# A gated-recurrence and expert-routing kernel: the path for very full experts as one loop, column numbers made a step before their conversion, and a fourth buffer of rows

## The chip, the cores and the metric

The kernel runs on one NeuronCore of a Trainium2 chip. The metric is device time in microseconds (us) of one execution, the median of three runs. The engines of the core are named as in the profile: PE is TensorE (PEld its weight loads), DVE VectorE, ACT ScalarE, POOL GpSimd, SP SyncE, which here issues most transfers. [...] records of a sequencer carry a q (PEq, ACTq).

## What is computed

Two stages follow each other. The first is a gated linear recurrence over 768 steps for 4 x 8 heads of 48 channels; the second routes each of the 3072 resulting rows of 384 values to one of 8 experts by cosine similarity, and applies that expert's two-layer network. The reference, cut to what matters:

```python
for t in range(S):                                   # B, H, S, D = 4, 8, 768, 48
    state = alpha[:, :, t, :, None] * state + einsum('bhd,bhe->bhde', k[:, :, t], v[:, :, t])
    y[:, :, t] = einsum('bhd,bhde->bhe', q[:, :, t], state)

x = y.transpose(0, 2, 1, 3).reshape(B * S, H * D)    # 3072 x 384
xn = x / (norm(x) + 1e-6);  en = expert_emb / (norm(expert_emb) + 1e-6)
logits = xn @ en.T / tau
expert_idx = argmax(logits, axis=1)                  # 8 experts
gate_w = softmax(logits)[arange(N), expert_idx]
for e in range(E):
    mask = expert_idx == e
    h = maximum(x[mask] @ w1[e], 0.0)                # 384 -> 1024
    out[mask] = gate_w[mask, None] * (h @ w2[e])     # 1024 -> 384
```

How many rows an expert gets depends on the data. With the reference's inputs the eight experts get 418, 365, 379, 426, 395, 371, 351 and 367 rows.

## The kernel before

The recurrence is done in 24 steps of 128 rows (`NS = 24`), software-pipelined over a loop `s`. Rows come out of step `s` two iterations later, are collected in tiles `x` for groups of one to three steps, get their expert (`choose`), their place in a list sorted by expert (`place`), and are sent to that list in DRAM by an indirect transfer from GpSimd (`to_rows`).

```python
    S0, EARLY = 16, 2
    # the groups of steps:
    # (0,3) (3,6) (6,9) (9,12) (12,14) (14,16) (16,19) (19,21) (21,23) (23,24)

    def routing_constants():
        nc.gpsimd.memset(ones, 1.0)
        make_upper_triangular(nc, earlier, val=1.0, diag=False)
        nc.gpsimd.iota(cols_i, pattern=[[1, E]], base=0, channel_multiplier=0)
        # ... three more iotas: toks_i, part_i, starts_i
        for f, i in ((cols, cols_i), (toks, toks_i), (part, part_i), (starts, starts_i)):
            nc.vector.tensor_copy(f, i)
        nc.vector.tensor_scalar(first, cols, -1.0, float(E), ALU.mult, ALU.add)
        nc.vector.tensor_scalar(ebase, cols, float(N), None, ALU.mult)
        nc.vector.tensor_scalar(before[:, 0], ebase, 1.0 / P, None, ALU.mult)
```

`before[:, s]` holds, per partition, how many rows of earlier steps chose each expert. `choose` ends with these additions; `place` multiplies them on TensorE (`rk`), and for steps 15 and 23 the total too:

```python
        def choose(g):
            # ... top, win, best and chosen, all on VectorE
            for s in range(s0, s1):
                eng = nc.vector if s == NS - 1 else nc.gpsimd
                eng.tensor_tensor(before[:, s + 1], before[:, s], chosen[:, s], ALU.add)

        def place(g, total=False):
            mm(rkf, lhsT=ones, rhs=before[:, s0:s1]..., start=True, stop=False)
            mm(rkf, lhsT=earlier, rhs=ch..., start=False, stop=True)
            if total:
                mm(bank[:, GMAX], lhsT=ones, rhs=before[:, s1], start=True, stop=True)
            # ... at_row, row and dest on VectorE

        def rows(s):
            # ... TensorE writes px, 128 rows of the step, into one of 3 PSUM buffers ("tr"),
            #     which the transposes pa, pk, pq, pkb of later steps use too
            if s == s0:
                x_g[g] = work.tile([P, GMAX, ROW], FP32, name="x", bufs=3)[:, 0 : s1 - s0]
            x = x_g[g][:, s - s0]
            nc.vector.tensor_reduce(x[:, LG : LG + E]..., px[...], axis=AX.XY, op=ALU.add)
            nc.scalar.copy(x[:, 0:DM]..., px[...])

        for s in range(NS + 3):
            # ... the work of the steps s, s - 1 and s - 2
            if s == 3:
                with behind(s):          # behind step s's second scan and its qs on GpSimd
                    routing_constants()
```

The experts then run one after another. Each has three blocks of 128 rows (`run`) and, if it has more than 384, a half block of 64 (`run_extra`, under a `tc.If`). Once, behind the fourth expert, stands a path for experts with more than 448 rows:

```python
        def half_block(w1_t, w2_t, xT, gate, col):
            # ... 48 matmuls ph, 8 matmuls pyo
            nc.scalar.copy(y[0:HALF], py[HALF:])
            nc.vector.tensor_tensor(y[0:HALF], y[0:HALF], py[0:HALF], ALU.add)
            nc.vector.tensor_scalar(y[0:HALF], y[0:HALF], gate, None, ALU.mult)
            scatter(y[0:HALF], col)

        def run_rest(free):
            w1_t, w2_t = w1_s[free], w2_s[free]
            big = nc.values_load(most, ...)          # half blocks over 384 of the fullest expert
            with tc.If(big > 1):
                for i in range(E):                   # eight copies in the program
                    e = nc.values_load(turn_i[0:1, i : i + 1], engines=(SP,), ...)
                    # ... load w1_t and w2_t of expert e
                    n = nc.values_load(extra[0:1, i : i + 1], ...)
                    with tc.For_i(1, n) as u:
                        # ... load 64 rows, transpose, gates
                        half_block(w1_t, w2_t, xT, gate[0:HALF], col[0:HALF])

        for i in range(E):
            # ... weights(i + 2) and fetch(i + 2)
            run(i)
            run_extra(i)
            if i == 3:
                run_rest(i % NW)
```

Of the kernel before, what the change touches and what calls it, by code (L numbers as in the profile page):

```python
# [9 lines left out]
FP32 = mybir.dt.float32  # L10
# [17 lines left out]
def kernel(  # L28
# [40 lines left out]

    xs = nc.dram_tensor("xs", (E * N + NROW, ROW), FP32, kind="Internal").ap()  # L70

    consts = ctx.enter_context(tc.tile_pool(name="consts", bufs=1))


# [36 lines left out]
# [4 lines that stand above are left out]
        nc.gpsimd.iota(toks_i, pattern=[[P, NS]], base=1, channel_multiplier=1)  # L115
        nc.gpsimd.iota(part_i, pattern=[[0, 1]], base=0, channel_multiplier=1)
        nc.gpsimd.iota(starts_i, pattern=[[P, NC + 1]], base=0, channel_multiplier=0)
        for f, i in ((cols, cols_i), (toks, toks_i), (part, part_i), (starts, starts_i)):
            nc.vector.tensor_copy(f, i)
        nc.vector.tensor_scalar(first, cols, -1.0, float(E), ALU.mult, ALU.add)  # L120
        nc.vector.tensor_scalar(ebase, cols, float(N), None, ALU.mult)
        nc.vector.tensor_scalar(before[:, 0], ebase, 1.0 / P, None, ALU.mult)
# [73 lines left out]
    with ExitStack() as c1:  # L196
# [123 lines left out]
        def choose(g):  # L320

            s0, s1 = GROUPS[g]
            n = s1 - s0
            shp = [P, n, E]
            l = x_g[g][:, :, LG : LG + E]
            top = work.tile([P, GMAX], FP32, name="top")[:, 0:n]
            nc.vector.tensor_reduce(top.unsqueeze(2), l, axis=AX.X, op=ALU.max)
            win = work.tile([P, GMAX, E], FP32, name="win")[:, 0:n]
            nc.vector.tensor_tensor(win, l, bc(top, shp, 2), ALU.is_equal)
            nc.vector.tensor_tensor(win, win, bc(first, shp, 1), ALU.mult)  # L330
            best = work.tile([P, GMAX], FP32, name="best")[:, 0:n]
            nc.vector.tensor_reduce(best.unsqueeze(2), win, axis=AX.X, op=ALU.max)  # L332
            ch = chosen[:, s0:s1]
            nc.vector.tensor_tensor(ch, win, bc(best, shp, 2), ALU.is_equal)
            for s in range(s0, s1):
                eng = nc.vector if s == NS - 1 else nc.gpsimd
                eng.tensor_tensor(before[:, s + 1], before[:, s], chosen[:, s], ALU.add)

        def place(g, total=False):
# [114 lines left out]
        def behind(s):  # L454

            queue = ExitStack()
            for call in st[s]["last"]:
                queue.enter_context(tc.issue_after(call.ins))
            return queue
# [149 lines left out]
        def rows(s):  # L609

            yT = st[s]["yT"]
            px = ps_tr.tile([P, 2, NQ, 2 * D + E], FP32, tag="tr", name="px")
            for hh in range(2):
                for q in range(NQ):

                    for i in range(2):
                        sl = slice(i * HALF, (i + 1) * HALF)
                        mm(
                            px[sl, hh, q], lhsT=yT[hh][:, q, sl], rhs=sel[:, hh, q],
                            start=True, stop=True, skip_group_check=True,  # L620
                        )
            g = group_of[s]
            s0, s1 = GROUPS[g]
            if s == s0:
                x_g[g] = work.tile([P, GMAX, ROW], FP32, name="x", bufs=3)[:, 0 : s1 - s0]
            x = x_g[g][:, s - s0]
            nc.vector.tensor_reduce(  # L627
                x[:, LG : LG + E].unsqueeze(2), px[:, :, :, 2 * D :].rearrange("t a q e -> t e a q"),
                axis=AX.XY, op=ALU.add,
            )  # L630
            nc.scalar.copy(  # L631
                x[:, 0:DM].rearrange("t (q j a d) -> t a q j d", q=NQ, j=2, a=2),
                px[:, :, :, 0 : 2 * D].rearrange("t a q (j d) -> t a q j d", j=2),
            )
# [36 lines left out]
        for s in range(NS + 3):  # L671
            if s + 2 <= NS:
                load(s + 2)
            if 0 <= s - 1 < NS:
                with in_turn():
                    keys_back(s - 1)
            if s < NS:
                decays(s)
            if s == NS:
                with in_turn():  # L680
                    turn_early()
            if s < NS:
                decay_queries(s)
            if 0 <= s - 1 < NS:
                decay_state(s - 1)

                with in_turn(), tc.issue_after(st[s]["a_scan"].ins) if s < NS else ExitStack():
                    scores(s - 1)
            if s == 0:
                with behind(s), in_turn():  # L690
                    prepare_first(a0)
                with behind(s):
                    prepare_logits()
            if NS <= s < NS + 2:
                with in_turn():
                    first_layer_early(2 * (s - NS), 2 * (s - NS) + 1)
            if 0 <= s - 2 < NS:
                with in_turn():
                    mix_states(s - 2)
                with in_turn():  # L700
                    mix_chunk(s - 2)
            if 0 <= s - 1 < NS:

                with in_turn(), tc.issue_after(st[s]["a_scan"].ins) if s < NS else ExitStack():
                    update(s - 1)
            if 0 < s < NS and s % NCH == 0:

                with in_turn():
                    keys_back(s, ps_mm, "mm")
            if NS <= s < NS + 2:  # L710
                with in_turn():
                    first_layer_early(2 * (s - NS) + 1, 2 * (s - NS) + 2)
            if 0 <= s - 2 < NS:
                with in_turn():
                    rows(s - 2)
            if s == 1:
                with in_turn():
                    turn_logits()
            if s == 3:
                with behind(s):  # L720
                    routing_constants()
            if 4 <= s < 4 + NXG * (NC + 1):
                i, t = divmod(s - 4, NC + 1)
                with behind(s):
                    nc.gpsimd.memset(xg_s[i][:, t], 0.0)
            if s == 3:
                with behind(s):
                    nc.gpsimd.memset(blank, 0.0)

            r = s - 3  # L730
            if r >= 0:
                g = group_of[r]
                if r == GROUPS[g][1] - 1:
                    with in_turn():
                        n = place(g, r in (S0 - 1, NS - 1))
                    if r == S0 - 1:
                        with behind(s):
                            first_expert(n)
            with behind(s) if s < NS else ExitStack():
                for c in send[:] if s >= NS else send[:1]:  # L740
                    to_rows(dest[:, c : c + 1], x_g[group_of[c]][:, c - GROUPS[group_of[c]][0]])
                    send.remove(c)
                    if c == S0 - 1:
                        fetch_early()
                        weights(0)
            if s == NS - 1:
                weights(1)
            r = s - 2
            if 0 <= r < NS:
                g = group_of[r]  # L750
                if r == GROUPS[g][1] - 1:
                    choose(g)
                    with behind(s) if s < NS else ExitStack():
                        nc.gpsimd.tensor_copy(x_g[g][:, :, TK], toks[:, slice(*GROUPS[g])])
            if s > NS:
                with in_turn():
                    first_layer_early(2 * (s - NS) + 2, 2 * (s - NS) + 4)
# [6 lines left out]
    with ExitStack() as c3:  # L764
# [164 lines left out]
        def run_rest(free):  # L929
# [4 lines left out]
                skip_runtime_bounds_check_because="the half blocks of an expert",  # L934
            )
            with tc.If(big > 1):  # L936
                for i in range(E):
                    e = nc.values_load(
                        turn_i[0:1, i : i + 1], engines=(SP,), min_val=0, max_val=E - 1,
                        skip_runtime_bounds_check_because="a sum of two experts, less E from E on",  # L940
                    )
                    nc.sync.dma_start(
# [3 lines left out]
                        out=w2_t, in_=w2_r[ds(e, 1)].rearrange("e p k d -> (e p) k d")  # L946
                    )
                    n = nc.values_load(
                        extra[0:1, i : i + 1], min_val=0, max_val=N // HALF - 2 * NC,
                        skip_runtime_bounds_check_because="the half blocks of an expert",  # L950
                    )
                    with tc.For_i(1, n) as u:
# [64 lines left out]
```

## Time and profile before

| | |
|---|---|
| time, median of 3 (lowest to highest) | 451.35 us (451.18 to 452.82) |
| span of the profiled execution | 451.3 us, granted TensorE clock 0.987 on average |
| DMA traffic | 60.10 MB, 133 GB/s over the span |
| matmuls of the experts, L843 and L854 | 120.8 + 115.6 us busy |
| VectorE's two scans in a step, L474 and L498 | 24 times 1.22 us each |
| GpSimd's scatter of 128 rows, L309 | 24 times 1.03 us |

The profile is one execution. Its page gives busy times by engine, the span in 40 equal slices (a digit is the busy share in tenths; PEclk is the clock that TensorE was granted, in tenths of full speed), the groups of instructions by source line, and the chain of work that ended last. The trace behind it can be asked who waited for whom, and for single instructions in order of time. A line such as `L936 ACTq COMPARE_BRANCH  x1: 45/45/45, 303.2 to 303.2` is a group of records: line, sequencer, operation, count, shortest/median/longest in ns, first and last start in us.

### The profile page before, as it was taken

What the parts mean: (1) busy time and instruction counts of PE and PEld (TensorE: products, weight loads), DVE (VectorE), ACT (ScalarE), POOL (GpSimd) and SP (SyncE); (2) the same over time, 40 slices, a digit from 0 to 9 for tenths busy, and PEclk for the clock granted to TensorE, in tenths of its full rate; (3) what the DMA queues carried; (4) which work ended last, traced back from release to release, by engine and by line L of the source; (5) the groups of instructions that cost most, each with busy time, mean ns of one, the idle gap of its engine ahead of it and who ended that gap; (6) DMA issues with size and microseconds to landing.
All of it is one profiled execution on the core that took longest, in us unless ns stands there. A gap on an engine that the chain in (4) does not pass through costs nothing.

```text
span 451.3 us, 9164 instructions
## 1 busy us (share of the span) xinstructions
PE 431.3 (96%) x3474; PEld 301.0 (67%) x3474; DVE 172.5 (38%) x464; ACT 154.7 (34%) x330; POOL 138.3 (31%) x230
## 2 busy tenths in 40 slices
PE   7989999999999999999999999988999999999992
PEld 6878888888788876765555555545556655655551
DVE  7878878788788344220211211110111121121010
ACT  4444444544454436622502413311421250250200
POOL 7455667676466445010010110102010001001010
PEclk9999999999999999999999999998999999999997
DMA  9999999999839825863045054008204500000000
GB/s 142 157 162 175 197 192 164 205 189 173 164 104 316 311 75 165 330 231 137 20 169 207 19 197 173 17 21 307 62 35 162 192 17 35 0 19 33 0 20 33
DMA packets 119369, 60.10 MB, mean 133 GB/s; under 512 B 102287, under 2 KB 113816, under 8 KB 119312
## 3 DMA queue, kind: packets, MB, share of 16 engines
q1 hardware_dynamic: 115208, 49.14, 46.9%
q0 software_dynamic: 3728, 10.16, 6.3%
q8 instruction: 34, 0.56, 0.5%
q14 instruction: 23, 0.19, 0.1%
q10 hardware_dynamic: 376, 0.05, 0.1%
HBM read 49.69 MB, written 11.45 MB: 135 GB/s over the span
## 4 chain that ended last, share of the span: by engine, by line
issue 53%; PE 26%; DVE 7%; POOL 5%; DMA 4%; another core or an unknown queue 2%; ACT 1%; POOLq 1%; DVEq 0%; ACTq 0%
PE pyx L187 6%; PE sc L187 4%; POOL out_dram L781 3%; PE px L187 3%; PE pyo L854 2%; PE pa L190 2%; PE pq L190 2%; PE pk L190 2%; PE pkb L190 2%; DVE r L474 2%; PE phe L187 2%; PE pd L187 1%; DMA xs<-x,dest 1%; DMA out_dram<-y,sx 1%
## 5 line engine op out<-in xcount | busy, mean ns | idle before, releaser
L843 PE MATMUL ph<-xT,w 128*128 128x384 f32 (+1 forms) x384 | 120.8, 466 | 3.8 <-ACTq L936 3.2
L854 PE MATMUL pyo<-w,hT 128*128 128x384 f32 x352 | 115.6, 488 | 0.0
L843 PEld LDWEIGHTS ph<-xT,w 128*128 128x128 f32 x384 | 68.4, 192 | 46.9 <-issue 5.7
L854 PEld LDWEIGHTS pyo<-w,hT 128*128 128x128 f32 x352 | 66.3, 190 | 45.3
L781 POOL DMA_INDIRECT out_dram<-y,sx x25 | 24.4, 977 | 229.3 <-DVE gt L824 135.2
L847 ACT ACTIVATE hT<-ph 128x384 f32<-128x384 f32 (+1 forms) x64 | 29.7, 465 | 141.4 <-PE ph L843 141.4
L797 DVE COPY xT<-pxg 128x384 f32<-128x384 f32 (+1 forms) x30 | 15.0, 504 | 95.5 <-PE pxg L796 95.5
L858 DVE TENSOR_SCALAR y<-pyo,gt 128x384 f32<-128x384 f32 (+1 forms) x22 | 13.4, 609 | 85.3 <-PE pyo L854 85.3
L502 POOL TENSOR_TENSOR qs<-qc,a 128x512 f32<-128x512 f32 x24 | 30.6, 1276 | 34.0 <-DVE a L498 24.1
L474 DVE TENSOR_TENSOR_SCAN r<-pa,inr 128x511 f32<-128x511 f32 x24 | 29.2, 1215 | 5.7 <-PE pa L190 5.5
L498 DVE TENSOR_TENSOR_SCAN a<-pa,ini 128x512 f32<-128x512 f32 x24 | 29.3, 1222 | 0.8
L309 POOL DMA_INDIRECT xs<-x,dest x24 | 24.8, 1032 | 11.2 <-DVE best L332 4.0
L187 PE MATMUL sc<-qs,kr 64*128 64x128 f32 x384 | 28.1, 286 | 0.0
L187 PE MATMUL pyx<-sm,vt 128*64 128x128 f32 x384 | 26.5, 279 | 0.2 <-POOL sm L568 0.2
L187 PEld LDWEIGHTS sc<-qs,kr 64*128 64x128 f32 x384 | 23.5, 189 | 4.2 <-issue 3.4
L187 PEld LDWEIGHTS pyx<-sm,vt 128*64 128x64 f32 x384 | 20.4, 136 | 4.4 <-issue 3.3
L607 ACT COPY ycols<-pyx 128x256 f32<-128x256 f32 x48 | 17.8, 374 | 13.9 <-PE pyx L187 12.5
L187 PE MATMUL px<-sel,ycols 128*64 128x104 f32 x384 | 21.5, 254 | 0.0
L484 ACT COPY qc<-pq 128x512 f32<-128x512 f32 x24 | 14.1, 586 | 21.2 <-PE pq L190 21.2
L631 ACT COPY x<-px 128x384 f32<-128x384 f32 x24 | 11.6, 484 | 25.5 <-DVE x L627 25.5
L567 ACT COPY sm<-sc 128x512 f32<-128x512 f32 x24 | 14.1, 587 | 13.5 <-PE sc L187 12.9
L187 PEld LDWEIGHTS px<-sel,ycols 128*64 128x64 f32 x384 | 17.7, 137 | 1.2 <-issue 0.7
(164 smaller groups left out, 504.4 us busy)
## 6 DMA issues: line engine op xcount, KB each, us to landing
w<-in_moe_w_dram SPq DMA_DIRECT2D x16, 1536.0 KB, 6.7
kt<-in_k_dram SPq DMA_DIRECT2D x24, 192.0 KB, 4.3
qt<-in_q_dram SPq DMA_DIRECT2D x24, 192.0 KB, 5.6
vt<-in_v_dram SPq DMA_DIRECT2D x24, 192.0 KB, 5.5
xg<-xs SPq DMA_DIRECT2D x22, 196.5 KB, 7.8
at<-in_alpha_dram SPq DMA_DIRECT2D x24, 168.0 KB, 5.7
xg<-xs SPq DMA_DIRECT2D x8, 98.2 KB
at<-in_alpha_dram SPq DMA_DIRECT2D x24, 22.5 KB, 5.2
```

What stands on the lines that cost most here:

```text
L187: last["pe"] = nc.tensor.matmul(*args, **kwargs)
L190: last["pe"] = nc.tensor.transpose(*args)
L309: ins = nc.gpsimd.indirect_dma_start(out=xs, out_offset=bass.IndirectOffsetOnAxis(ap=rows, axis=0), in_=x, in_offset=None, bounds_check=E ...
L474: nc.vector.tensor_tensor_scan(r[:, L - 2 :: -1], pa[:, L - 1 : 0 : -1], inr[:, L - 2 :: -1], 1.0, ALU.mult, ALU.add,)
L498: d["a_scan"] = by_dve = nc.vector.tensor_tensor_scan(a, pa, ini, 0.0, ALU.mult, ALU.add)
L502: by_pool = nc.gpsimd.tensor_tensor(qs.rearrange("p n t -> p (n t)"), d["qc"], a, ALU.mult)
L607: nc.scalar.copy(yT[hh].rearrange("p q t -> p (q t)"), pyx[hh][:, 0:YX])
L781: ins = nc.gpsimd.indirect_dma_start(out=out, out_offset=bass.IndirectOffsetOnAxis(ap=col, axis=0), in_=y, in_offset=None, bounds_check=N - 1,
L797: return nc.vector.tensor_copy(xT, px[:, :, 0:n])
L843: nc.tensor.matmul(ph, lhsT=w1_t[:, i, f * P : (f + 1) * P], rhs=xT[:, i], start=(i == 0), stop=(i == KT - 1),)
L847: return nc.scalar.activation(hT[:, f], ph, AF.Relu)
L854: nc.tensor.matmul(py, lhsT=hT[:, f], rhs=w2_t[:, f], start=(f == 0), stop=(f == FT - 1),)
```

## The change

There are four parts. The path for experts with very many rows becomes one run-time loop over the experts (`tc.For_i`) in place of eight copies in the program; [...] `extra` and `turn_i` are first written to DRAM, and each pass loads its two numbers from there. GpSimd's numbering of the columns (`iota`) is issued one step ahead of VectorE's conversion to float, so that VectorE need not wait for it. The addition that feeds the total after step 15 goes to VectorE. And the tile of rows `x` has four buffers in place of three, so that a group need not wait for the scatter of the group three before it.

```diff
+    turns = nc.dram_tensor("turns", (2, E), I32, kind="Internal").ap()
...
         nc.gpsimd.iota(starts_i, pattern=[[P, NC + 1]], base=0, channel_multiplier=0)
+
+    def convert_constants():
         for f, i in ((cols, cols_i), (toks, toks_i), (part, part_i), (starts, starts_i)):
             nc.vector.tensor_copy(f, i)
...
-                eng = nc.vector if s == NS - 1 else nc.gpsimd
+                eng = nc.vector if s in (S0 - 1, NS - 1) else nc.gpsimd
...
-                x_g[g] = work.tile([P, GMAX, ROW], FP32, name="x", bufs=3)[:, 0 : s1 - s0]
+                x_g[g] = work.tile([P, GMAX, ROW], FP32, name="x", bufs=4)[:, 0 : s1 - s0]
...
+            if s == 2:
+                with behind(s):
+                    routing_constants()
             if s == 3:
                 with behind(s):
-                    routing_constants()
+                    convert_constants()
...
             with tc.If(big > 1):
-                for i in range(E):
+                nc.sync.dma_start(out=turns[0:1], in_=extra)
+                nc.sync.dma_start(out=turns[1:2], in_=turn_i)
+                with tc.For_i(0, E) as i:
+
+                    cur = yp.tile([1, 2], I32, name="cur", bufs=1)
+                    for j in range(2):
+                        nc.sync.dma_start(
+                            out=cur[0:1, j : j + 1], in_=turns[j : j + 1, ds(i, 1)]
+                        )
                     e = nc.values_load(
-                        turn_i[0:1, i : i + 1], engines=(SP,), min_val=0, max_val=E - 1,
+                        cur[0:1, 1:2], engines=(SP,), min_val=0, max_val=E - 1,
...
                     n = nc.values_load(
-                        extra[0:1, i : i + 1], min_val=0, max_val=N // HALF - 2 * NC,
+                        cur[0:1, 0:1], min_val=0, max_val=N // HALF - 2 * NC,
```

## The prediction

> **What bounds the kernel now.** I read the shares and the slices of the page first, then the waits of TensorE, then TensorE's work around each gap.
>
> ```profile
> PE 431.3 (96%) x3474; PEld 301.0 (67%) x3474; DVE 172.5 (38%) x464; ACT 154.7 (34%) x330; POOL 138.3 (31%) x230
> ...
> PE   7989999999999999999999999988999999999992
> ...
> DVE  7878878788788344220211211110111121121010
> ...
> PEclk9999999999999999999999999998999999999997
> ```
>
> TensorE is busy 431.3 of 451.3 us, so at most 20.0 us of gaps can be won without touching its matmuls. The change touches no matmul that runs. Two places matter: the first third, where VectorE stands at 7 and 8 beside a TensorE at 9, and the two slices from 293 to 316 us where TensorE drops to 8, in the second of them its clock too. A count of the 20.0 us by stretch: 2.8 before 12 us (start), 8.7 after 443 us (last scatter and end), 3.2 at 302 us, and the rest in the recurrence. The waits of TensorE, whole span (engine, line, who was waited for; us in total, times, longest):
>
> ```profile
> PE ph L843 <- ACTq L936: 3.2, 1, 3.2
> PE pk L190 <- ACT x L631: 2.2, 2, 1.3
> PE rk L187 <- DVE x L627: 1.8, 2, 0.9
> ...
> PE rk L187 <- POOL before L337: 0.8, 1, 0.8
> ...
> PE pyx L187 <- POOL sm L568: 0.2, 1, 0.2
> ```
>
> Line 936 is the `tc.If` around the path for experts with very many rows. The reference's inputs give the experts 418, 365, 379, 426, 395, 371, 351 and 367 rows; `most` is then ceil((426 - 384) / 64) = 1, the condition `big > 1` is false, and the whole path is jumped over once. Not one instruction of it runs. The jump costs the largest single wait of TensorE. The sequencers' own records at that line:
>
> ```profile
> L936 ACTq EVENT_SEMAPHORE  x2: 17/17/17, 305.7 to 305.8; - x2
> L936 DVEq EVENT_SEMAPHORE  x2: 21/21/21, 309.1 to 309.2; - x2
> ...
> L936 PEldq COMPARE_BRANCH  x1: 3447/3447/3447, 300.5 to 300.5; - x1
> L936 ACTq COMPARE_BRANCH  x1: 45/45/45, 303.2 to 303.2; - x1
> L936 DVEq COMPARE_BRANCH  x1: 56/56/56, 304.4 to 304.4; - x1
> ```
>
> ScalarE branches at 303.2, but its next instruction, the semaphore that lets TensorE go, comes at 305.7: 2.5 us for one jump. VectorE needs 4.7 us, and TensorE's branch itself takes 3.4. A branch over an unused half block (line 923) is the comparison: TensorE 0.07 to 0.35 us, ScalarE from branch to semaphore 0.5 us (253.0 to 253.5), VectorE 0.2 to 0.3. The difference is the distance. By the two built programs, the long jump passes 712 instructions of TensorE, 290 of ScalarE and 337 of VectorE; that of a half block 58, 5 to 9 and 4. What follows the gap, weight loads in order of time:
>
> ```profile
> 305.74 0.30 PEld L843 LDWEIGHTS ph<-xT,w 128*128 128x128 f32 x2 [3.83 <-ACTq L936]
> 306.26 0.34 PEld L843 LDWEIGHTS ph<-xT,w 128*128 128x128 f32 x1 [0.23 <-issue]
> ```
>
> They come 0.64 us apart until 309.46, then 0.32 to 0.34 us. The granted clock in 306.0 to 309.5 is 0.51, and 1.00 on both sides. So the gap has a tail: 3.41 us at half speed.
>
> [...] The trace [...] shows blocks of two sizes: queue q8 34 packets with 0.56 MB, 16 KB each, and q14 23 with 0.19 MB, 8 KB each. [...] half speed for 3.41 us behind a gap of 3.16 us, and none behind the gaps of 1.33, 0.90 and 0.88 us. [...]
>
> **The change, part by part.**
>
> (1) The loop over experts. The eight bodies become one, so the same jump passes 117 instructions on TensorE, 66 on ScalarE, 71 on VectorE, 62 on GpSimd, 94 on SyncE. The new copies `turns` and `cur` stand inside the jumped part and cost nothing here. TensorE's 117 are about twice a half block's 58, which never stalled in five jumps[...]. I take the jump as a near one. TensorE's last matmul before it ends at 302.58. The semaphore of ScalarE remains, because the code behind the If waits for ScalarE's count, and ScalarE must first do its copy (302.66 + 0.48 = 303.14) and branch (303.2). With 0.5 us of near jump it comes at 303.7 in place of 305.74. The gap goes from 3.16 to 1.15 us: **2.0 us**. A gap of 1.15 us is smaller than the 1.33 us that left the clock alone, so the half-speed stretch goes as well: 3.41 us of it did 1.7 us of work, which saves **1.7 us**.
>
> (2) Numbering one step earlier. The chain before:
>
> ```profile
> 24.16 0.26 POOL qs L502
> 24.42 0.96 issue
> 25.38 0.21 POOL ones L112
> ...
> 25.73 0.10 POOL cols_i L114
> ...
> 27.07 0.32 DVE state L552
> 27.39 0.11 DVE x L627
> ...
> 27.52 0.50 ACT x L631
> ...
> 28.07 0.66 PE pk L190 x4
> ```
>
> VectorE ends its second scan at 24.03 and `sm` at 24.61, then stands 1.26 us for `cols_i`, because GpSimd writes it only behind `qs`. Everything after is late: `state`, `x`, the copy of `x` on ScalarE, and with it the PSUM buffer that `pk` needs. With the numbers written a step earlier the seven conversions (0.65 us to `first`, some 0.5 us for the last two) lie on both sides of `sm` (the order in the built program); `state` then starts near 25.8, `x` near 26.1, ScalarE's copy ends near 26.8, and `pa` ends at 26.74. `pk` starts at 26.8 instead of 28.07: **1.27 us**. GpSimd's 1.0 us of numbering moves before `sm` of step 2, which then ends near 21.9; its reader starts at 23.44. Hidden.
>
> (3) The addition for row block 15 on VectorE. `rk` of the total waits 0.79 us (from 117.27 to 118.06) because GpSimd does that addition behind a scatter (116.75, 1.01 us). On VectorE it takes about 0.17 us, as the one at 163.8 does, and can start at 116.6, when GpSimd's addition for block 14 is done. It is ready before TensorE asks: **0.79 us**; VectorE's 0.17 us is hidden, since VectorE stood 1.67 us in front of `at_row`.
>
> (4) The fourth buffer of rows. GpSimd waits 4.43 us (150.79 to 155.22) for a scatter to give back a buffer. TensorE feels 0.20 us of it, at 159.01: **0.2 us**.
>
> Sum: 2.0 + 1.7 + 1.27 + 0.79 + 0.2 = 6.0 us, 451.35 - 6.0 = 445.4. I keep 0.1 back for places where another engine comes second: 445.5.
>
> **The rivals.** (a) The short jump stalls too. For: nothing in the trace shows a jump of ScalarE over 66 instructions, only 5 to 9[...]. Against: the half block of TensorE, 224 and more instructions once each matmul is its two loads and two matmuls, [...] cost 0.35 us at most. Then only parts 2 to 4 remain: 449.1. (b) The gap shrinks but the clock still drops[...]: 447.1. (c) The loads set the pace of the recurrence, and its 2.3 us come back as waits for q, k, v or alpha. For: the DMA row stands at 9 in the first twelve slices. Against: TensorE waited only once for a load, 0.5 us, while SyncE waited for TensorE to free buffers (10.1 us at line 452 alone). 447.7. (d) VectorE's `sm`, 0.7 us later in step 3, delays the next step's matmuls; its reader comes 5 us later, so I give it little: 446 to 447. [...]
>
> **Range and chances.** (a) about one in eight, (b) one in ten, some loss as in (c) or (d) one in four. The range is 443.7 to 448.6. Two per cent are 9.0 us, more than the sum and nearly all gaps outside start and end (8.5 us), so faster by over 2% gets 0.03; for 2% slower nothing speaks, 0.01.
>
> **What would show it.** Right: the wait of `ph` for ScalarE's sequencer near 1.1 us, all engines' branch to semaphore at that line below 1 us, no half clock after 13 us, no wait of `pk` at 27 us, no wait of `rk` for GpSimd, no wait of GpSimd for a scatter at 151 us, and TensorE's busy time down by about 1.7 us. Wrong: a wait above 2 us at the jump (a), a granted clock of 0.5 behind it (b), TensorE waiting for loads (c), or the two waits for `x` at 56 and 92 us growing (d).

## The result, and the profile after

The changed kernel takes 447.5 us (median of four runs, 447.15 to 447.95); the kernel before, run beside it, 452.09 us (four runs, 451.18 to 452.83). The ratio is 0.990, with a 95% interval of 0.9874 to 0.9926: the change saves between 0.7% and 1.3%. The predicted time was 445.5 us, with a range of 443.7 to 448.6 us. The span of the profiled execution went from 451.3 to 445.5 us, a difference of 5.8 us against the 6.0 us of the sum. The saving was nearly the one that was worked out, but it lies in other places.

The page of the changed kernel, first the shares, then the slices:

```profile
PE 427.9 (96%) x3474; PEld 299.1 (67%) x3474; DVE 173.3 (39%) x465; ACT 154.3 (35%) x330; POOL 137.7 (31%) x229
...
PE   6989999999989999999999999999999999999992
...
DVE  7888878788888343321211211211111121121010
...
PEclk9999999999999999999999999999999999999997
```

The two slices between 293 and 316 us in which TensorE stood at 8 are 9 now, and the clock in them as well. TensorE's busy time fell by 3.4 us, twice what was expected. Half of that is the stretch at half clock behind the jump. The other half is a stretch at half clock from 9.1 to 12.5 us, which the execution of before had and this one has not; it was worth nothing, because the transpose `pa` of step 4 starts at 26.14 us in both.

The waits of TensorE, whole span (engine, line, who was waited for; us in total, times, longest):

```profile
PE pk L194 <- ACT x L635: 2.3, 2, 1.2
PE rk L191 <- DVE x L631: 1.8, 2, 0.9
...
PE ph L850 <- PEq L943: 0.4, 1, 0.4
```

Line 943 is now the `tc.If`. Its wait fell from 3.2 to 0.4 us, and its releaser is TensorE's own sequencer, no longer ScalarE's. The wait of `rk` for GpSimd has gone. The two waits of `pk` for ScalarE's copy of `x` have not: 2.2 us before, 2.3 us after. That is the first sign that part 2 brought next to nothing.

Each engine's sequencer branches for itself, TensorE's at 299.2 us, ScalarE's at 301.8 and VectorE's at 303.0. Their records at the jump (count; shortest, median, longest in ns; first and last start):

```profile
L943 PEldq EVENT_SEMAPHORE  x2: 51/51/51, 301.3 to 301.4; - x2
L943 ACTq EVENT_SEMAPHORE  x2: 17/17/17, 302.3 to 302.4; - x2
L943 DVEq EVENT_SEMAPHORE  x2: 21/21/21, 303.6 to 303.7; - x2
...
L943 PEldq COMPARE_BRANCH  x1: 424/424/424, 299.2 to 299.2; - x1
L943 ACTq COMPARE_BRANCH  x1: 45/45/45, 301.8 to 301.8; - x1
L943 DVEq COMPARE_BRANCH  x1: 56/56/56, 303.0 to 303.0; - x1
```

TensorE's branch took 0.42 us instead of 3.45, ScalarE came from branch to semaphore in 0.5 us instead of 2.5, VectorE in 0.6 instead of 4.7. The timeline of TensorE there (start, us, engine, line, operation):

```profile
301.69 2.82 PE L850 MATMUL ph<-xT,w 128*128 128x384 f32 x8 [0.45 <-PEq L943]
```

TensorE restarts at 301.69 us, before ScalarE's semaphore at 302.3. It does not wait for ScalarE at all, which no step of the prediction had. Granted clock and work of TensorE behind the jump, in before and then in the changed kernel (stretch; its length, busy time and matmuls, clock, share of the DMA engines, GB/s):

```profile
306.00:309.50 3.50, 3.50 (x7) 0.51 0.90 348
```

```profile
306.00:309.50 3.50, 3.50 (x13) 1.00 1.02 387
```

In before this stretch held 7 matmuls at a clock of 0.51; now it holds 13 at 1.00.

Setting the same instructions of both traces side by side shows where the 5.8 us came from. The column is how far the later kernel is ahead.

| at | ahead, us | what was gained just before |
|---|---|---|
| `pa` of step 4 (26.1 us) | 0.0 | the start |
| `pa` of step 5 (33.3) | 0.19 | part 2 |
| `pa` of step 19 (117.1) | 1.17 | part 3: 0.98 |
| `pa` of step 21 (129.6) | 0.84 | 0.33 given back at 124.7 |
| `pa` of step 23 (142.0) | 0.91 | 0.07, of no part |
| first `ph` of the experts (178.2) | 1.33 | part 4 and the end of the recurrence: 0.42 |
| first `ph` behind the jump (301.7) | 4.05 | the gap at the jump: 2.72 |
| `ph` of the next block (306.0) | 5.78 | the half clock behind it: 1.73 |

### The profile page after: what moved, and what is told of

It is laid out like the page before. It is cut to its first block, busy times and chain, and to the rows that moved or that the text cites. A ratio compares the mean times of both kernels' runs of the same rounds, so it can differ in the third digit from the quotient of the medians.

```text
span 445.5 us, 9144 instructions
## 1 busy us (share of the span) xinstructions
PE 427.9 (96%) x3474; PEld 299.1 (67%) x3474; DVE 173.3 (39%) x465; ACT 154.3 (35%) x330; POOL 137.7 (31%) x229
## 5 line engine op out<-in xcount | busy, mean ns | idle before, releaser
L850 PE MATMUL ph<-xT,w 128*128 128x384 f32 (+1 forms) x384 | 119.1, 462 | 1.0 <-PEq L943 0.4
L635 ACT COPY x<-px 128x384 f32<-128x384 f32 x24 | 11.6, 484 | 25.8 <-DVE x L631 25.8
```

Source lines behind the costliest of these rows:

```text
L850: nc.tensor.matmul(ph, lhsT=w1_t[:, i, f * P : (f + 1) * P], rhs=xT[:, i], start=(i == 0), stop=(i == KT - 1),)
```

## The experiments

There are ten runs, each beside runs of the kernel before. Five of the kernels have a single time; what is concluded from them is read from their traces.

### The loop alone, and the rest without the loop

The first kernel is the kernel before with part 1 only:

```diff
-                for i in range(E):
-                    e = nc.values_load(turn_i[0:1, i : i + 1], ...)
+                nc.sync.dma_start(out=turns[0:1], in_=extra)
+                nc.sync.dma_start(out=turns[1:2], in_=turn_i)
+                with tc.For_i(0, E) as i:
+                    cur = yp.tile([1, 2], I32, name="cur", bufs=1)
+                    # ... load cur from turns[:, i]
+                    e = nc.values_load(cur[0:1, 1:2], ...)
```

> The kernel before with the loop over the experts alone. In the two traces the jump's gap fell from 3.16 to 0.45 us and the 3.41 us of half clock behind it went (1.7 us of work): if the loop is the cause of both, the gap is 0.45 us again, no half clock lies behind it, and the span falls by 4.4 us against a run of before that shows the half clock at the jump, by about 2.7 us against one that does not. Rival (the gain comes from the other three parts[...]): the gap shrinks to some 0.5 us but the time falls by less than 2 us.

Measured: 448.73 us (four runs, 448.5 to 449.93), ratio 0.9907 (0.9877 to 0.9936). That is 4.2 us below the median of before, 452.9 us, where 4.4 were expected of the span. The execution profiled is the one of 449.93 us, which is 1.0 us behind the changed kernel already at `pa` of step 4 (27.15 us), long before the jump. The second kernel has parts 2 to 4 and keeps the eight copies:

```diff
-            if s == 3:
+            if s == 2:
                 with behind(s):
                     routing_constants()
+            if s == 3:
+                with behind(s):
+                    convert_constants()
 ...
-                eng = nc.vector if s == NS - 1 else nc.gpsimd
+                eng = nc.vector if s in (S0 - 1, NS - 1) else nc.gpsimd
 ...
-                x_g[g] = work.tile([P, GMAX, ROW], FP32, name="x", bufs=3)...
+                x_g[g] = work.tile([P, GMAX, ROW], FP32, name="x", bufs=4)...
```

> The kernel after with the eight copies of before, so parts 2 to 4 alone. Expected from the marks in the two traces: 0.2 us from the numbering, 0.65 us from the addition on VectorE, 0.4 us from the fourth buffer, together 1.3 us; the gap at the jump stays near 3.2 us. The rival says 3 us or more, because the prediction's 1.27 us of part 2 would come back in another run.

Measured: 451.52 us (17 runs, 450.94 to 452.84), ratio 0.9978 (0.9965 to 0.999), so 0.1% to 0.35%. The loop makes most of the saving, and the other three parts together 0.5 to 1.6 us, where 1.3 were expected. The waits of TensorE with the loop alone, then those without the loop:

```profile
PE rk L189 <- POOL before L339: 0.8, 1, 0.8
PE ph L845 <- PEq L938: 0.4, 1, 0.4
```

```profile
PE ph L848 <- ACTq L941: 3.5, 1, 3.5
PE pk L192 <- ACT x L633: 2.0, 2, 1.2
```

With the loop alone the gap is 0.45 us, and the wait of `rk` for GpSimd, which belongs to part 3, stays. Without the loop the jump stalls as it did, and the clock drops for longer (stretches as above):

```profile
303.10:306.50 3.40, 2.26 (x4) 0.50 0.81 237
306.50:309.90 3.40, 3.40 (x7) 0.50 1.01 384
```

### Why the gap fell below what was predicted: the buffer behind the jump

In the kernel before, two things end only after TensorE's last matmul ahead of the jump (302.58 us): TensorE's own branch, at 303.94 us, and ScalarE's semaphore, at 305.7. The built programs tell why ScalarE matters. The first matmul behind the path takes one of the four PSUM buffers `ph` in rotation. With eight copies, that buffer was last used inside the jumped path, so the matmul waits for a count of ScalarE (270) that ScalarE only reaches by jumping too. With one body, which uses two buffers, its last user is the block ahead of the `If` (count 228), which is long done. Two runs separate the two. The first is the kernel before with its eight copies, whose half blocks share two PSUM buffers taken before the copies, so that the wait for ScalarE goes and the long jump stays:

```diff
+                phs = [ps_h.tile([P, 512], FP32, name="ph") for _ in range(2)]
 ...
-                ph = ps_h.tile([P, 512], FP32, name="ph")[:, 0 : 4 * HALF]
+                ph = (phs[f0 // 4] if phs else ps_h.tile([P, 512], FP32, name="ph"))[:, 0 : 4 * HALF]
```

> The kernel before, its eight copies and all distances of the jump kept, but the half blocks of the skipped path share two PSUM tiles ph instead of taking sixteen. Then the first matmul behind the path no longer waits for ScalarE's count from inside the path (270, now 228), as in the kernel after. If ScalarE's late jump held TensorE, it now starts when its own jump is over, near 304.1 by the trace of before: a gap of about 1.5 us and perhaps no half clock. If TensorE's own second instruction block (a 16 KB transfer from 304.6 to 305.7 in that trace) held it, the gap stays at 3.0 to 3.2 us.

Measured: 450.29 us (one run). The records of the sequencers, and the timeline:

```profile
L936 PEldq EVENT_SEMAPHORE  x2: 51/51/51, 304.4 to 304.5; - x2
L936 ACTq EVENT_SEMAPHORE  x2: 17/17/17, 305.6 to 305.7; - x2
...
L936 PEldq COMPARE_BRANCH  x1: 3863/3863/3863, 300.5 to 300.5; - x1
```

```profile
304.79 2.17 PE L843 MATMUL ph<-xT,w 128*128 128x384 f32 x6 [2.25 <-PEq L936]
```

TensorE starts 0.8 us before ScalarE's semaphore, with a gap of 2.25 us that lies between the two expectations. So in before it was ScalarE's semaphore that came last. How the 3.16 us divide is known less well, because TensorE's branch took 3.86 us in this run and 3.45 in before. By the gaps as they are, 0.9 us were the wait for ScalarE beyond TensorE's own jump, 1.8 the long jump of TensorE itself, and 0.45 stay with the short one; with the branch as long as in before the first two are an estimated 1.3 and 1.4. The granted clock behind this gap was 1.00.

The second is the changed kernel whose body in the loop uses four buffers in place of two:

```diff
-            for f0 in range(0, FT, 4):
-                ph = ps_h.tile([P, 512], FP32, name="ph")[:, 0 : 4 * HALF]
+            for f0 in range(0, FT, fs):          # fs = 2 in the path, 4 elsewhere
+                ph = ps_h.tile([P, 512], FP32, name="ph")[:, 0 : fs * HALF]
```

> The kernel after, with the skipped path's half block in four PSUM tiles ph of half the width instead of two. The distances of the jump hardly change (119 instructions of TensorE for 117, 68 of ScalarE for 66), but the first matmul behind it again waits for ScalarE's count from inside the path (235 against 230 counted outside). If that wait is what the rotation of the tiles makes of it, the gap grows from 0.45 to about 1.1 us, as ScalarE's semaphore came 1.06 us after the last matmul before the jump in the trace of after; if the wait plays no part it stays at 0.45 us.

Measured: 449.25 us (one run), and this wait:

```profile
PE ph L850 <- ACTq L943: 1.1, 1, 1.1
```

The wait for ScalarE is back, at 1.12 us. It is the 1.15 us that the prediction had for the changed kernel, with ScalarE's near jump in it; only the buffers' rotation made the difference.

### How far a jump may go

The changed kernel with four bodies, each in a loop over two experts:

```diff
-                with tc.For_i(0, E) as i:
+                for c0 in range(0, E, 2):
+                    with tc.For_i(c0, c0 + 2) as i:
```

> The kernel after, with the skipped path as four loops over two experts each: the jump passes 468 instructions of TensorE and 258 of ScalarE, in place of 117 and 66 (after) or 712 and 290 (before), and the matmul behind it waits for ScalarE's count from inside (246 against 230). [...] TensorE's branch takes about 3 us as in before and ScalarE's semaphore 2 us or more after its branch: gap 2.3 to 3.3 us. If the stall grew with the length in proportion, the gap would be near 1.6 us; if only the wait for ScalarE mattered, 1.1 us as with the four tiles.

Measured: 451.31 us (one run).

```profile
L943 ACTq EVENT_SEMAPHORE  x2: 17/17/17, 304.0 to 304.1; - x2
...
L943 PEldq COMPARE_BRANCH  x1: 3407/3407/3407, 298.9 to 298.9; - x1
L943 ACTq COMPARE_BRANCH  x1: 45/45/45, 301.6 to 301.6; - x1
```

The gap was 3.11 us, and ScalarE's semaphore ended it; a stretch of half clock of 3.4 us begins 0.4 us before that end. TensorE's branch over 468 instructions takes 3.41 us here, and over 712 it took 3.45 in before; over 117 it takes 0.42. On ScalarE 258 and 290 instructions cost 2.4 and 2.5 us, and 66 cost 0.5. So the stall did not grow in proportion to the distance: it was small at the shorter distances, and whole at both of the longer ones. Where the step lies between 117 and 468, or between 66 and 258, was not measured.

The traces also show transfers of instructions (in before, the page's queues of kind `instruction`: q8 with 16 KB a packet, q14 with 8 KB). In all four traces with the long jump TensorE's branch ends 1.35 to 1.37 us after a block of 16 KB has landed (302.57 and 303.94 us in before). That transfer took 1.00 to 1.42 us, and the branches of 3.41, 3.45, 3.74 and 3.86 us differ by little else: 2.41 to 2.45 us are left without it. In the seven traces with the short jump the branch is over before the block at that place begins to move (299.59 and 300.36 us in the changed kernel). An 8 KB block lands between ScalarE's branch and its semaphore in the four with the long jump (304.64 us in before), and in none of the others. So the long branch goes with such a transfer, and the short one is over without it; what starts a transfer, and what the other 2.4 us are, was not shown.

How much is left to win at this place is shown by the kernel before without the path. It leaves out the rows over 448 of an expert, of which these inputs have none:

```diff
-            if i == 3:
-                run_rest(i % NW)
```

> The kernel before with the path for very full experts left out of the program altogether; with these inputs it never runs, with fuller experts rows would be missing. No jump there: TensorE should have a gap of at most 0.15 us at that place and no half clock, so the span is 3.2 us plus the half clock's 1.7 us below that of before, and some 0.4 us below what the loop gives.

Measured: 448.13 us (one run), no gap at that place and no half clock there. Against the changed kernel it gains 0.5 us across the jump: the loop leaves just its 0.45 us gap to be won.

### Why part 2 brought little: VectorE is held beside GpSimd

The timeline of the changed kernel in step 3, VectorE and GpSimd, and the late matmul:

```profile
24.19 0.14 DVE L123 CAST cols<-cols_i 128x8 f32<-128x8 int32 x1
...
24.42 1.27 POOL L506 TENSOR_TENSOR qs<-qc,a 128x512 f32<-128x512 f32 x1 [2.00 <-DVE cols L123]
24.46 1.62 DVE L124 TENSOR_SCALAR first<-cols 128x8 f32<-128x8 f32 x1
...
25.63 0.43 POOL L735 MEMSET blank<- 128x393 f32 x1
25.63 0.68 DVE L570 TENSOR_TENSOR sm<-sc,causal 128x512 f32<-128x512 f32 x1
...
26.78 0.43 DVE L556 TENSOR_TENSOR state<-pd,dec 128x256 f32<-128x256 f32 x1
...
27.34 0.49 ACT L635 COPY x<-px 128x384 f32<-128x384 f32 x1 [2.38 <-DVE x L631]
...
27.88 0.66 PE L194 MATMUL pk<-ident,kt 128*128 128x128 f32 x4 [1.14 <-ACT x L635]
```

The conversions do start at once, at 24.19 us instead of 25.86. But `first`, 8 numbers in a row, takes 1.62 us: it starts 0.04 us after GpSimd's `qs` and ends at 26.08, 0.02 us after GpSimd's memset. Meanwhile `sm`, which stands behind it, starts at 25.63 instead of 23.94, and `state` at 26.78 instead of 26.98. So `first` ended with GpSimd's work, while `sm` ran beside the memset in 0.68 us, against 0.67 in the steps before and after. Why GpSimd's work holds the one and not the other is not in the trace.

Which instruction is held differs between executions. In the traces of two other kernels with the same order here (the one without the loop, and the one with four bodies) `first` takes 0.17 us, although `qs` had started 0.04 us before it. `qs` takes 1.35 us there in place of 1.27, and it is `ebase`, behind `sm`, that is held, 1.02 and 1.03 us, until just after the memset. `pk` then waits 0.80 us, and step 4 is 0.5 us shorter than in before, not 0.19 as here. So part 2 is worth 0.2 to 0.5 us in the traces kept. Two runs tell whether it is GpSimd's nearness or VectorE's work that makes part 2 fail. In the first, the conversions are put where GpSimd is idle, right behind VectorE's `kr` of step 3:

```diff
-            nc.vector.tensor_tensor(krf, pk, r, ALU.mult)
+            d["by_kr"] = nc.vector.tensor_tensor(krf, pk, r, ALU.mult)
 ...
+            if s == 3:
+                with tc.issue_after(st[s]["by_kr"].ins):
+                    convert_constants()
             if s < NS:
                 decay_queries(s)
 ...
-            if s == 3:
-                with behind(s):
-                    convert_constants()
```

> The kernel after, with VectorE's seven conversions issued behind kr of step 3, where GpSimd stands idle before qs, and not behind the second scan, where GpSimd runs qs. Theory: the conversions lost their time because VectorE was held while GpSimd ran qs and the memset behind it (first took 1.62 us and ended 0.02 us after that memset, sm came 1.4 us late). Then first takes under 0.4 us, the copy of x on ScalarE ends near 26.8 us, TensorE's gap before pk of step 4 falls from 1.14 us to under 0.3 us, and every later mark of TensorE comes about 1 us earlier (time about 446.5 us against 447.5). Rival: seven more instructions on VectorE in that step are too many wherever they stand; then the gap keeps at 0.8 us or more.

Measured: 446.49 us (four runs, 446.2 to 446.7), ratio 0.9867 (0.9843 to 0.989). The same stretch:

```profile
22.18 0.20 POOL L511 TENSOR_TENSOR end<-r,al 128x4 f32<-128x4 f32 x1
...
22.59 0.16 DVE L123 CAST cols<-cols_i 128x8 f32<-128x8 int32 x1
...
22.87 0.16 DVE L124 TENSOR_SCALAR first<-cols 128x8 f32<-128x8 f32 x1
...
23.14 0.17 DVE L126 TENSOR_SCALAR before<-ebase 128x8 f32<-128x8 f32 x1
...
26.03 0.49 ACT L635 COPY x<-px 128x384 f32<-128x384 f32 x1 [1.03 <-DVE x L631]
...
26.62 0.61 PE L194 MATMUL pk<-ident,kt 128*128 128x128 f32 x4
```

Between GpSimd's `end` at 22.18 and its `qs` at 24.60 us, all seven take 0.15 to 0.17 us each, 0.7 us from first to last. `pk` starts at 26.62 without a gap, and every mark from step 6 to the end stands 1.15 to 1.17 us earlier than in the changed kernel. That is what part 2 was to bring. VectorE has free time at this place too, since its second scan starts only 0.18 us later than in the changed kernel (23.23 and 23.05 us); that the hold is the larger part is read from the durations, 0.16 us against 1.62.

In the second, ScalarE makes the seven constants by copies, from numberings that GpSimd writes directly:

```diff
-            nc.vector.tensor_copy(f, i)
-        nc.vector.tensor_scalar(first, cols, -1.0, float(E), ALU.mult, ALU.add)
+            nc.scalar.copy(f, i)
+        nc.scalar.copy(first, first_i)      # and ebase, before[:, 0] likewise
```

> The kernel after, with the conversions on ScalarE (seven copies of small tables, first, ebase and the first column of before numbered by GpSimd as integers too). VectorE has nothing to convert then. If holding by GpSimd is the cause, ScalarE is not held and each copy takes 0.2 us; the gap of 1.14 us before pk of step 4 falls under 0.5 us. If ScalarE's own queue becomes the late one (seven copies are 1.4 us in front of its copy of x), the gap stays near 1 us with ScalarE as the one waited for.

Measured: 447.95 us (one run). The waits of TensorE:

```profile
PE px L197 <- ACT ycols L617: 2.0, 1, 2.0
...
PE pk L200 <- ACT x L641: 1.2, 1, 1.2
```

The wait of `pk` at 28 us went, and only the one at 125 us is left. But the first copy came to stand ahead of a copy of `ycols` at 20 us, before GpSimd had written `cols_i`: ScalarE stood 2.26 us for it, and `px` behind waited 1.96 us for `ycols`. The wait for `cols_i` was moved to another engine. The run shows that ScalarE's copies take 0.20 us each beside GpSimd, but not what they would bring at a better place.

### The two waits of `rk`, and the better version

With part 2 working, the two largest gaps of the recurrence that are left alone are `rk` for VectorE's `x`, 0.88 and 0.89 us at 55 and 91 us. This run puts `place`, with its matmuls `rk`, behind the next step's decays, for the groups that end before step 20 other than that of step 15:

```diff
+        waiting, LATE = None, 20
 ...
             if s < NS:
                 decays(s)
+            if waiting is not None:
+                with in_turn():
+                    place(waiting)
+                waiting = None
 ...
-                if r == GROUPS[g][1] - 1:
+                if r == GROUPS[g][1] - 1 and r < LATE and r != S0 - 1:
+                    waiting = g
+                elif r == GROUPS[g][1] - 1:
```

> The kernel of the conversions behind kr (446.49 us, span 444.3), with one thing more: the numbering of the rows' places (place) of the groups that end before step 20, other than that of step 15, is put behind the decays of the next step, so that its matmuls rk come to TensorE when VectorE has freed their PSUM bank. Theory (the two waits of rk at 56 and 92 us, 0.88 and 0.89 us in the changed kernel, are TensorE coming too early for a bank that VectorE frees later, and nothing needs rk at once): both waits are gone, about 1.7 us less, span near 442.6, time near 444.8 us. Rival (the waits are only the place where VectorE's lateness is felt, and it is felt at the next read instead): the waits turn up under other names within the same or the next step, time 446.2 to 446.8 us.

Measured: 446.65 us (four runs, 446.23 to 447.06), ratio 0.9864 (0.9824 to 0.9904): no gain over the version without the shift. The waits of TensorE:

```profile
PE pk L194 <- ACT x L635: 1.9, 3, 1.2
...
PE phe L191 <- DMA w<-in_moe_w_dram: 0.9, 1, 0.9
```

The rival was half right. In place of two waits of 0.88 us for `rk` there are two of 0.37 us for `pk`. The recurrence was 1.1 us ahead at the matmuls `sc` of step 23, and then lost 0.9 us in a wait for the first expert's weights, and 0.4 us more at the branch of a half block (line 937). The issues of those loads on SyncE, in this kernel and in the one without the shift:

```profile
L141 SPq DMA_DIRECT2D w<-in_moe_w_dram x2: 383/2892/5401, 137.5 to 138.9; - x2
```

```profile
L141 SPq DMA_DIRECT2D w<-in_moe_w_dram x2: 383/1903/3423, 131.9 to 133.3; - x2
```

They are asked for 5.6 us later, because SyncE stands in line 181 for the scatter of the rows of steps 16 to 18, which the shift had delayed. So the last run shifts only the groups that end before step 14:

```diff
-        waiting, LATE = None, 20
+        waiting, LATE = None, 14
```

> As the run before (place behind the decays of the next step), but only for the groups that end before step 14, so that the scatter of steps 16 to 18 goes out as early as it did. In the run before, the recurrence was 1.1 us ahead at the scores of step 23 and lost 0.9 us at once, because SyncE waited for that scatter to 136.4 us (131.0 us without the shift) and the first expert's weights behind it were asked for at 137.5 us instead of 131.9 us. Theory (that late scatter alone took the gain back): no wait of TensorE for w at 148 us, weights asked for before 132 us, and about 1.0 us of the gain stays: span near 443.4, time near 445.5 us. Rival (something else between 147 us and the end would take it): the wait for w gone, but time 446.3 to 446.8 us.

Measured: 445.68 us (four runs, 445.58 to 445.91), ratio 0.9836 (0.982 to 0.9853). The waits of TensorE that are left there:

```profile
PE pk L194 <- ACT x L635: 1.9, 3, 1.2
PE pw L191 <- POOL ident masks.py:199: 1.6, 1, 1.6
...
PE ph L857 <- PEq L950: 0.4, 1, 0.4
```

The wait for `w` is gone, and the marks stand 1.84 us ahead of the changed kernel from the matmuls `sc` of step 16 to the end. This version beats both kernels: its interval ends below that of the changed kernel. Its four times also lie below the four of the version without the shift, by 0.8 us in the median.

## Why the prediction was right in sum and wrong in parts

**(1) The loop.** Right that the short jump is a near one on every engine (0.42 us for TensorE's branch, 0.2 to 0.6 us from branch to semaphore on the others), that the gap shrinks and that the half clock goes with it: 1.73 us, as said. That it would be a near one was an estimate of mine, from the half block's 0.07 to 0.35 us on TensorE and 0.5 us on ScalarE. Wrong in "The semaphore of ScalarE remains, because the code behind the If waits for ScalarE's count". It waits for whatever count the buffer's last user left, and the loop changed that user. The gap became 0.45 us in place of 1.15, and the term 2.72 us in place of 2.0. The run with four buffers, 1.12 us, shows that the rest of the step's arithmetic held. Of the gain of 2.72, 1.4 to 1.8 was TensorE's own jump, which the step had hidden behind ScalarE's.

**(2) The numbering.** The step that failed is "the seven conversions (0.65 us to `first`, some 0.5 us for the last two) lie on both sides of `sm` (the order in the built program); `state` then starts near 25.8". It started at 26.78, and 0.19 us came of 1.27 (0.5 in the two other traces). The step took the time of the wait for `cols_i` away and left out whom the conversions would then run beside. The sign was in the trace of before: there the same `toks`, 0.17 us in the changed kernel, took 0.53 us, from 25.96 to 26.49, beside GpSimd's memset that ended at 26.45. I read those durations as the cost of the conversions. The position behind `kr` shows that the mechanism (a late `x` holds the buffer that `pk` needs) was right, and the 1.16 us it brings near the 1.27 worked out.

**(3) The addition.** The wait of 0.79 us for GpSimd went and the mark shows 0.98 us. Then 0.33 us came back at the next step, where `pk` waits for the copy of `x` 1.16 us in place of 0.83. The changed kernel, and then the same operation in before:

```profile
117.58 0.64 POOL L572 TENSOR_SCALAR_AFFINE_SELECT sm<-sm 128x512 f32<-128x512 f32 x1
...
117.61 0.63 DVE L377 SCALAR_TENSOR_TENSOR ok<-n,first 128x8 f32<-128x8 f32 x1
...
124.72 0.66 PE L194 MATMUL pk<-ident,kt 128*128 128x128 f32 x4 [1.16 <-ACT x L635]
```

```profile
118.78 0.16 DVE L373 SCALAR_TENSOR_TENSOR ok<-n,first 128x8 f32<-128x8 f32 x1
```

The earlier `rk` put VectorE's `ok`, again 8 numbers a row, beside GpSimd's `sm`; in before it came after that `sm` had ended. So VectorE starts `at_row` 1.17 us earlier than in before, but its next scan `r` only 0.81 us earlier, and TensorE, 1.17 us ahead, waits for what is missing. All eight traces with the addition on VectorE show `ok` at 0.63 or 0.64 us, and all four without it at 0.16. No run moved `ok` alone. The prediction had counted the 0.17 us of the addition, and not what the rest of the chain would then run beside. The net is 0.65 us against 0.79.

**(4) The fourth buffer.** GpSimd's wait of 4.43 us for a scatter and TensorE's 0.20 us at 159 us are gone; GpSimd stands 2.9 us there for ScalarE's copy of `x` instead, which TensorE does not feel. From the last step to the first expert 0.42 us were gained against 0.2; which of the rest belongs to this part was not separated.

Together, with the 0.07 that belongs to no part: 2.72 + 1.73 + 0.19 + 0.65 + 0.07 + 0.42 = 5.8 us. That this is so near the 6.0 of the sum was luck: 0.7 us too little for the gap and 1.1 too much for part 2 went opposite ways.

**The absolute time.** Of the miss of 2.0 us, 1.55 lies in the base. The profiled execution of before took 452.98 us, but the sum was taken from 451.35, the median of three runs. Over the 20 runs of before beside the first experiments the median is 452.9 us, and the times fall in groups: three at 451.2 to 451.4, fourteen at 452.7 to 453.3, three at 454.0 to 454.4. Subtracting 6.0 from 452.9 gives 446.9; 447.5 was measured. The 1.6 us between the first two groups go with the mean granted clock: over all 41 runs of before beside the experiments it is 0.994 to 0.997 in the seven under 452 us, and 0.984 to 0.992 in the other 34. The half clock behind the jump costs 1.7 us, so the lower group may be the executions that escape it; the sum would then have taken 1.7 us for a half clock from a time that had none. No trace of such an execution was kept, and the mean also takes in half clock at the start and the end of the span, so this is not shown. The time outside the span went from 1.7 to 2.1 us. That goes with the loop: 1.9 to 2.1 us in the four runs of the loop alone, and 1.7 to 1.85 in the 17 runs of the other parts without it. Why is open, and one run with the loop (the copies on ScalarE) has 1.75.

**The rivals.** (a) a short jump that stalls and (b) a clock that still drops did not occur in the changed kernel: the gap was 0.45 us and the clock behind it 1.00. (c) came true in part: TensorE waits 1.8 us for q and k there, and 0.5 in before, but all of it before 16 us, and by `pa` of step 4 nothing of it is left. Only in the run with the late scatter did a load take a gain, 0.9 us. (d) named VectorE's `sm`, but with the wrong size: it is 1.7 us later, not 0.7, and it was what stands behind it, `state` and `x`, that TensorE felt.

## What to carry to other kernels

A path that the data never takes still costs its jump, on each engine (on TensorE 3.45 us over 712 instructions here, 0.42 over 117), and its buffers still take part in the rotation (1.12 us of gap with four buffers, 0.45 with two): make the body small, and ask which wait the first instruction behind it inherits. Before an operation is moved earlier, look at what its engine's neighbour does at the new time, since a duration from the old place is not its cost; on VectorE what GpSimd did beside it counted (`first` 1.62 us against 0.16), not only the order. When one wait is removed, follow what its engine issues next (here a scatter, then a queue of weight loads), because that is where the gain can be lost again.

## What the runs showed of the hardware that was not expected

A VectorE instruction on 8 numbers a row took 0.16 us where GpSimd was idle, and 1.62 us where GpSimd's `qs` and memset ran. Another took 0.16 us, and 0.63 beside GpSimd's `sm`. The hold reached the instruction queued behind it, too (`sm` started at 25.63 us in place of 23.94), and which instruction it met differed between executions (`first` for 1.62 us in one, `ebase` for 1.02 and 1.03 us in two others).

The cost of a jump had a step in it rather than a slope: TensorE's branch took 0.42 us over 117 instructions, 3.41 over 468 and 3.45 to 3.86 over 712. On VectorE, with the eight copies, it was 4.7, 3.1 and 2.9 us in three traces.

The clock stayed at 1.00 behind a gap of 2.25 us, and fell to 0.50 for one stretch of 3.41 us at gaps of 3.11 and 3.16 us and for two such stretches at one of 3.47 us. The traces tell more than the gaps. The half clock began 0.31 us behind the gap in before, but 0.4 us ahead of its end with the four bodies and 1.15 us ahead of it without the loop. In the 3.41 us up to its start TensorE was busy 0.31 us in before (302.64 to 306.05), 0.68 with the four bodies (300.30 to 303.71) and 1.09 without the loop (299.68 to 303.09). There the first stretch at half clock had 2.26 us busy, and a second one followed. Which length of a gap brings the half clock, between 2.25 and 3.11 us, and whether its place counts as well, was not shown.
